# Own buffers for the second layer's sums and the last results, and the next pair's factors prepared later

## The chip, the core and the metric

The kernel runs on one core of a Trainium2 chip. The metric is the device time of one execution in microseconds (us). Five engines take part, each with its own queue of instructions that it works off in order: TensorE (PE, matrix products, with its weight loads shown as PEld), VectorE (DVE), ScalarE (ACT), GpSimd (POOL) and SyncE (SP), whose queue issues most of the transfers. They meet only at semaphores: an instruction that waits holds up everything behind it on its engine.

## What is computed

```python
def _attn_ref(q, k, v, omega):            # Performer attention, 4 batches, 8 heads, 576 x 64
    q_p, k_p = (phi(q * scale), phi(k * scale))      # random features, exp
    kv = np.einsum('bhsm,bhsd->bhmd', k_p, v)
    num = np.einsum('bhsm,bhmd->bhsd', q_p, kv)
    den = np.einsum('bhsm,bhm->bhs', q_p, np.sum(k_p, axis=2))[..., None] + 1e-06
    return num / den

def _moe_ref(x, w_in, w_out):             # layer one, 2304 tokens, 512 -> 2048 -> 512
    h = x @ w_in
    return (h * np.clip(h + 3.0, 0.0, 6.0) / 6.0) @ w_out

def _moe2_ref(x, w_in, w_out):            # layer two, same sizes
    h = x @ w_in
    return (h / (1.0 + np.exp(-1.702 * h))) @ w_out
```

The result is layer two of layer one of the attention's output.

## The kernel before

All products are in float32, each factor split into a high and a low part: a "split" is a cast on ACT (the high part) and a subtraction on DVE or POOL (the low part), and every product of two factors is then three matmuls. Attention of one batch runs beside layer one of the batch before it. Layer one writes its result to `xs` in DRAM; layer two reads it from there. The change lies in layer two and in the preparation of its input.

**Layer two, first half (`h_pair`).** The four batches are worked on in two pairs. For each pair, the product with the 2048 columns of `w_in` is made in eight steps (u = 0 to 7), each by Strassen's scheme: seven products instead of eight, `product(op, ...)` with op 1, 6, 2, 5, 7, 3, 4 in this order, of six matmuls each. Their left factors (sums and differences of weight blocks) come from DRAM through the six buffers `wss`; their right factors `xo` are sums and differences of blocks of the input, split. Four PSUM banks take a step's products: b1 (op 1, then op 2), b6 (op 6), b5 (op 5, then op 3), b7 (op 7, then op 4). Steps alternate between the two groups of four banks, `acc` and `psp`. DVE adds them up (L856): u2, t, and the sums c22, c12 and c21. `gated` (L863, L864) makes the activation of a block: a sigmoid on ACT, then a product on POOL for c22, c12 and c21, on DVE for b1. The results g stay in SBUF.

**Layer two, second half (`o_block`).** For each of the pair's two batches, 16 chunks of 128 rows of g are split (`halves`: L931 on ACT, L932 on DVE) into a buffer `gs`, and twelve matmuls for each chunk (L921) add to four banks (`o`); the first batch of a pair uses the banks `acc`, the second `psp`. At the end of a block `evict` brings the banks to SBUF and they are sent out. The last block of the program also does the rest, 64 rows of each batch that do not fill a tile: two banks more, which are evicted first, in halves of 128 KB.

**Buffers.** A pool's tag is a ring of buffers: a new tile of a tag waits until the readers of the tile that held its buffer are done. The tag `gs` of the pool `gp`, three buffers, holds the chunks' splits, and also c22, c12 and c21 of every step of `h_pair`. The pool `lp` has a tag `gs` too, three buffers, which only the rest's smaller splits use. `evict` takes its buffer from `ga` (three) and `ob` (two) in turn.

**The next pair's factors (`x_ops`).** While the first pair's `o_block`s run, 16 steps prepare the second pair's xo: for each of two halves q a load of two tiles `xr` from `xs` (a ring of two buffers, so the second load waits for the first half's last readers), and seven parts in the order op 1, 2, 3, 7, 6, 5, 4. A part of op 7, 6, 5 or 4 makes its sum in place on POOL (L615 to L621), and then splits it: L623 on ACT, L624 on DVE. `side` takes one step after each chunk.

**What sets the order.** The instructions are written in the order of the Python code, but a scheduler then places them, engine by engine, by its own estimate of when each can run: an instruction that is ready early moves ahead. So the place of a split or a matmul in its queue follows from when its buffer comes free. Transfers of weights for later items (`fetch_to`, L757 and L760) are issued from SP, up to five items ahead.

Of the kernel before, what the change touches and what calls it, by code (L numbers as in the profile page):

```python
# [22 lines left out]
def performer_moe_kernel(  # L23
# [23 lines left out]
    SM = R * P  # L47
# [513 lines left out]

    n_out = [0]

    def evict(ps, sc, wide):
        n_out[0] += 1
        k = n_out[0]
        tag, bufs = ("ga", 3) if wide and k % 2 else ("ob", 2)
        ob = gp.tile([P, SM], F32, tag=tag, bufs=bufs, name="ob")
        if k % 2:
            nc.vector.tensor_scalar(out=ob, in0=ps, scalar1=sc, scalar2=None, op0=ALU.mult)  # L570
        else:
            nc.scalar.activation(out=ob, in_=ps, func=AF.Copy, scale=sc)
        return ob
# [15 lines left out]
    def x_ops(p, pool, tag):  # L589

        raw = {}
        room = {}

        def place(k):
            if 4 <= k < 10:
                return lp.tile([P, 2, SM], F32R, tag=f"xo{k - 4}", name="xo")
            if k in (0, 10):
                room[k] = xp_.tile([P, 4, 2, SM], F32R, tag="x", bufs=2, name="xo")
            return room[0][:, k] if k < 4 else room[10][:, k - 10]

        def load(q):
            for e in range(2):
                t = raw[q, e] = pool.tile([P, 2, SM], F32, tag=tag, bufs=2, name="xr")
                nc.sync.dma_start(
                    out=t, in_=xs[2 * p + e].rearrange("(h q) p s -> q p h s", q=2)[q]
                )

        def part(q, k, op):
            (b11, b21), (b12, b22) = (
                (raw[q, e][:, 0], raw[q, e][:, 1]) for e in range(2)  # L610
            )
            add = nc.gpsimd.tensor_tensor
            src = {1: b11, 2: b21, 3: b22, 7: b12, 6: b11, 5: b12, 4: b21}[op]
            if op == 7:
                add(out=b12, in0=b22, in1=b12, op=ALU.subtract)  # L615
            elif op == 6:
                add(out=b11, in0=b12, in1=b11, op=ALU.add)
            elif op == 5:
                add(out=b12, in0=b22, in1=b11, op=ALU.subtract)
            elif op == 4:  # L620
                add(out=b21, in0=b21, in1=b11, op=ALU.subtract)  # L621
            s = xop[q, op] = place(k)
            nc.scalar.copy(s[:, 0], src)  # L623
            nc.vector.tensor_tensor(out=s[:, 1], in0=src, in1=s[:, 0].bitcast(F32), op=ALU.subtract)  # L624

        order = (1, 2, 3, 7, 6, 5, 4)
        steps = []
        for q in range(2):
            steps.append(lambda q=q: load(q))
            steps += [lambda q=q, k=k: part(q, 7 * q + k, order[k]) for k in range(7)]  # L630
        return steps

    omt = const.tile([P, M], F32, name="omt")
# [104 lines left out]
    def side():  # L738
        pace[1] += 1
        if pace[1] % 2:  # L740
            return
        while todo and (pace[0] - len(todo)) * 4 * NC < pace[0] * pace[1]:
            todo.pop()()
# [69 lines left out]
    def h_pair(p, u):  # L813
# [35 lines left out]
        def bank():  # L849
            return psum.tile([P, SM], F32, tag=tag, name="h")  # L850

        def temp(tag, bufs, name):
            return gp.tile([P, SM], F32, tag=tag, bufs=bufs, name=name)

        def add(out, a, b):
            nc.vector.tensor_tensor(out=out, in0=a, in1=b, op=ALU.add)  # L856
# [10 lines left out]
        w["a"] = next_item()  # L867
        b1, b6 = bank(), bank()
        product(1, "a", 0, b1, True)
        p1 = temp("ga", 3, "p1")  # L870
        nc.scalar.copy(p1, b1)
        w["d"] = next_item()
        product(6, "d", 0, b6, True)
        u2 = temp("ga", 3, "u2")
        add(u2, p1, b6)
        product(2, "a", 1, b1, False)
        gated(0, b1, nc.vector)
# [3 lines left out]
        w["c"] = next_item()  # L881
        b5, b7 = bank(), bank()
        product(5, "c", 1, b5, True)
        t = temp("ga", 3, "t")
        add(t, u2, b5)
        product(7, "c", 0, b7, True)
        c22 = temp("gs", 3, "c22")
        add(c22, t, b7)
        product(3, "d", 1, b5, False)
        c12 = temp("gs", 3, "c12")  # L890
        add(c12, u2, b5)
        w["b"] = next_item()
        gated(2, c12, nc.gpsimd)
        gated(3, c22, nc.gpsimd)
        product(4, "b", 1, b7, False)
        c21 = temp("gs", 3, "c21")
        add(c21, u2, b7)
        gated(1, c21, nc.gpsimd)
        if last:
# [11 lines left out]
    def o_block(p, e, side):  # L911
# [23 lines left out]
        for c in range(NC):  # L935
            w = next_item()
            if left:
                s = halves(lp, B * SL, gl[c // 4][:, c // 2 % 2, c % 2])
                for d in range(B * SL // P):
                    rows(s, w, pl[d], d, c)  # L940
                    if c == NC - 1:
                        ob = evict(pl[d], 1.0, True)
                        for k, eng in enumerate((nc.sync, nc.scalar)):
                            r0 = (2 * d + k) * S + SM
                            eng.dma_start(out=out[r0:r0 + SL, :], in_=ob[k * SL:(k + 1) * SL, :])
            s = halves(gp, SM, gt[c // 2, e][:, c % 2])
            for d in range(SM // P):
                rows(s, w, ps[d], d, c)
                if c == NC - 1:
                    ob = evict(ps[d], 1.0, True)  # L950
                    nc.sync.dma_start(out=out[i * S + d * P:i * S + (d + 1) * P, :], in_=ob)
            side()
# [8 lines left out]
    for p in range(B // 2):  # L961
# [4 lines left out]
        if p + 1 < B // 2:  # L966
            prep = x_ops(p + 1, l1, "xr") + [left_x]

        def side():
            if prep:  # L970
                prep.pop(0)()

        for e in range(2):
# [60 lines left out]
```

## Time and profile before

| | |
|---|---|
| median of 3 runs | 958.74 us (958.34 to 961.16) |
| the profiled execution, its own time | 957.59 us |
| its span, first to last instruction | 955.8 us |
| PE busy | 931.8 us, 97% of the span |
| DVE, ACT, POOL busy | 523.6, 441.8 and 261.9 us |
| mean granted TensorE clock | 0.995 of full speed |

The profiled execution takes 1.8 us more than its span, and 1.15 us less than the median. PE is busy nearly all the time, so time can only be lost where PE stands still, where its clock falls, or before its first and after its last matmul. Matmul durations overlap (one is shown with some 0.39 us, and starts follow each other at 0.23 us), so the pace is read from a stretch of many.

### The profile page before, as it was taken

What the parts mean: (1) busy time and instruction counts of PE and PEld (TensorE: products, weight loads), DVE (VectorE), ACT (ScalarE), POOL (GpSimd) and SP (SyncE); (2) the same over time, 40 slices, a digit from 0 to 9 for tenths busy, and PEclk for the clock granted to TensorE, in tenths of its full rate; (3) what the DMA queues carried; (4) which work ended last, traced back from release to release, by engine and by line L of the source; (5) the groups of instructions that cost most, each with busy time, mean ns of one, the idle gap of its engine ahead of it and who ended that gap; (6) DMA issues with size and microseconds to landing.
All of it is one profiled execution on the core that took longest, in us unless ns stands there. A gap on an engine that the chain in (4) does not pass through costs nothing.

```text
span 955.8 us, 14633 instructions
## 1 busy us (share of the span) xinstructions
PE 931.8 (97%) x5566; PEld 764.7 (80%) x5566; DVE 523.6 (55%) x879; ACT 441.8 (46%) x904; POOL 261.9 (27%) x223
## 2 busy tenths in 40 slices
PE   8899999999999999999999999998999999999997
PEld 7777777778887888878888888876888888878885
DVE  7888889587574766547554234448232433342221
ACT  5887676576553765636443233344222323232221
POOL 0112223055342454516441005346000233210000
PEclk9999999999999999999999999998999999999999
DMA  5668578688776786756553257674576555466531
GB/s 189 227 230 277 211 258 311 232 292 296 234 284 247 243 295 238 265 199 248 212 199 114 88 176 258 210 231 182 197 235 205 176 176 176 158 197 203 170 111 66
DMA packets 62101, 203.47 MB, mean 213 GB/s; under 512 B 6736, under 2 KB 8400, under 8 KB 62032
## 3 DMA queue, kind: packets, MB, share of 16 engines
q1 hardware_dynamic: 61872, 202.28, 62.0%
q8 instruction: 44, 0.72, 0.3%
q10 hardware_dynamic: 160, 0.26, 0.1%
q14 instruction: 25, 0.20, 0.1%
HBM read 155.85 MB, written 46.66 MB: 212 GB/s over the span
## 4 chain that ended last, share of the span: by engine, by line
PE 81%; DVE 9%; ACT 5%; DMA 2%; issue 1%; POOL 1%; SPq 0%; ACTq 0%; DVEq 0%; POOLq 0%
PE o L921 19%; PE ps L495 17%; PE o L545 17%; PE h L823 16%; PE ps L250 3%; DVE w L200 2%; PE hl L840 2%; PE ps L383 1%; PE ps L347 1%; POOL w L193 1%; ACT e L258 1%; ACT wtop L176 1%; DVE xo L624 1%; PE ps L369 1%; DVE mx L256 1%
## 5 line engine op out<-in xcount | busy, mean ns | idle before, releaser
L921 PE MATMUL o<-wss,gs 128*128 128x512 f32 x864 | 200.7, 394 | 5.8 <-ACT gs L931 4.7
L921 PEld LDWEIGHTS o<-wss,gs 128*128 128x128 f32 x864 | 163.5, 190 | 43.0 <-ACT gs L931 5.6
L823 PE MATMUL h<-xo,wss 128*128 128x512 f32 x672 | 159.0, 393 | 0.0
L545 PE MATMUL o<-gs,wss 128*128 128x512 f32 (+1 forms) x660 | 150.5, 375 | 1.5 <-ACT gs L511 1.5
L495 PE MATMUL ps<-x,wss 128*128 128x512 f32 x576 | 145.8, 398 | 2.2 <-DVE x L240 0.7
L823 PEld LDWEIGHTS h<-xo,wss 128*128 128x128 f32 x672 | 124.5, 188 | 26.9
L193 POOL TENSOR_TENSOR w<-w,wpow 128x512 f32<-128x512 f32 x64 | 76.0, 1208 | 234.9 <-DVE wpow L188 152.7
L545 PEld LDWEIGHTS o<-gs,wss 128*128 128x128 f32 x660 | 112.4, 188 | 22.7 <-ACT gs L511 2.9
L495 PEld LDWEIGHTS ps<-x,wss 128*128 128x128 f32 x576 | 104.2, 188 | 26.1 <-ACT wss L203 1.6
L864 POOL TENSOR_TENSOR g<-g,c 128x512 f32<-128x512 f32 x48 | 63.6, 1329 | 175.7 <-ACT g L863 175.2
L932 DVE TENSOR_TENSOR gs<-g,gs 128x512 fp32r<-128x512 f32 x64 | 48.6, 764 | 102.0 <-ACT gs L931 101.7
L507 DVE SCALAR_TENSOR_TENSOR ga<-ga,ps 128x512 f32<-128x512 f32 (+1 forms) x80 | 49.9, 628 | 86.4 <-ACT ga L506 86.2
L931 ACT CAST gs<-g 128x512 fp32r<-128x512 f32 x64 | 39.6, 621 | 108.0 <-PE o L921 104.8
L506 ACT ACTIVATE ga<-ps,three 128x512 f32<-128x512 f32 (+1 forms) x80 | 51.8, 651 | 74.4 <-PE ps L495 74.4
L200 DVE TENSOR_TENSOR w<-w,wtop 128x512 f32<-128x512 f32 x64 | 70.0, 1106 | 20.9 <-POOL w L193 20.5
L258 ACT ACTIVATE e<-ps,mx 128x128 f32<-128x128 f32 x220 | 62.9, 396 | 19.1 <-DVE mx L256 19.1
L545 PE MATMUL o<-gs,wsh 128*128 128x512 f32 (+1 forms) x300 | 68.8, 376 | 1.2 <-ACT gs L511 1.2
L512 DVE TENSOR_TENSOR gs<-ga,gs 128x512 fp32r<-128x512 f32 (+1 forms) x80 | 59.2, 754 | 19.5 <-ACT gs L511 18.3
L863 ACT ACTIVATE g<-c 128x512 f32<-128x512 f32 x48 | 30.3, 632 | 73.1 <-DVE c L856 73.1
L545 PEld LDWEIGHTS o<-gs,wsh 128*128 128x128 f32 x300 | 51.4, 188 | 11.2 <-ACT gs L511 1.4
L511 ACT CAST gs<-ga 128x512 fp32r<-128x512 f32 (+1 forms) x80 | 45.9, 582 | 16.1 <-DVE ga L507 15.9
L220 POOL TENSOR_TENSOR wsn<-w,wsn 128x512 fp32r<-128x512 f32 x32 | 42.7, 1334 | 31.4 <-ACT wsn L219 31.4
(152 smaller groups left out, 1204.1 us busy)
## 6 DMA issues: line engine op xcount, KB each, us to landing
wss<-ws1o SPq DMA_DIRECT2D x64, 512.0 KB, 3.3
wss<-ws0i SPq DMA_DIRECT2D x36, 512.0 KB, 4.9
wss<-ws0o SPq DMA_DIRECT2D x33, 512.0 KB, 4.8
wraw<-in_w_in_dram SPq DMA_DIRECT2D x32, 512.0 KB, 4.6
wraw<-in_w_out_dram SPq DMA_DIRECT2D x32, 512.0 KB, 5.7
ws1o<-wsn SPq DMA_DIRECT2D x16, 512.0 KB, 3.5
wss<-sumsa SPq DMA_DIRECT2D x16, 512.0 KB, 3.4
wss<-sumsd SPq DMA_DIRECT2D x16, 512.0 KB, 3.7
```

The costliest lines, as they stand in the source:

```text
L193: nc.gpsimd.tensor_tensor(out=w[:, cols], in0=w[:, cols], in1=q[:, cols], op=ALU.mult)
L200: nc.vector.tensor_tensor(out=wj, in0=wj, in1=a[:, j * DM:(j + 1) * DM], op=ALU.add)
L258: act = nc.scalar.activation(out=e[:, r, :], in_=ps[:, r, :], func=AF.Exp, bias=mx[:, r:r + 1])
L495: nc.tensor.matmul(out=ps, lhsT=w[:, wi, kk, :], rhs=x[:, xi, kk, :], start=(m == 0), stop=(m == 3 * NK - 1),)
L506: nc.scalar.activation(out=g, in_=ps, func=AF.Relu, bias=three)
L507: nc.vector.scalar_tensor_tensor(out=g, in0=g, scalar=6.0, in1=ps, op0=ALU.min, op1=ALU.mult)
L512: gate[1] = nc.vector.tensor_tensor(out=s[:, 1, :], in0=g, in1=s[:, 0, :].bitcast(F32), op=ALU.subtract)
L545: nc.tensor.matmul(out=ps[:, e, :], lhsT=w[:, wi, cols], rhs=s[:, gi, :], start=(c == 0 and m == 0 and per == 1), stop=(c == NC - 1 and m ...
L823: nc.tensor.matmul(out=ps, lhsT=s[:, wi, q, :], rhs=xop[q, op][:, xi], start=(first and m == 0), stop=(m == 5), skip_group_check=not first,)
L864: eng.tensor_tensor(out=g, in0=g, in1=src, op=ALU.mult)
L921: nc.tensor.matmul(out=ps, lhsT=s[:, gi, d * P:(d + 1) * P], rhs=w[:, wi, :], start=(c == 0 and m == 0), stop=(c == NC - 1 and m == 2),)
L932: nc.vector.tensor_tensor(out=s[:, 1], in0=g, in1=s[:, 0].bitcast(F32), op=ALU.subtract)
```

## The change

The three sums c22, c12 and c21 take their buffers from the tag `gs` of `lp` instead of that of `gp`. The rest's two results take theirs from `lp`'s tags `xo0` and `xo1` (factors that are no longer read then) instead of `ga` and `ob`. In `x_ops` a sum on POOL is written one step ahead of the split that uses it, and `side` lets two chunks pass before its first step.

```diff
-    def evict(ps, sc, wide):
+    def evict(ps, sc, wide, home=None):
         n_out[0] += 1
         k = n_out[0]
-        tag, bufs = ("ga", 3) if wide and k % 2 else ("ob", 2)
-        ob = gp.tile([P, SM], F32, tag=tag, bufs=bufs, name="ob")
+        if home is not None:
+            ob = lp.tile([P, SM], F32, tag=home, name="ob")
+        elif wide and k % 2:
+            ob = gp.tile([P, SM], F32, tag="ga", bufs=3, name="ob")
+        else:
+            ob = gp.tile([P, SM], F32, tag="ob", bufs=2, name="ob")
...
-        def part(q, k, op):
-            (b11, b21), (b12, b22) = (
-                (raw[q, e][:, 0], raw[q, e][:, 1]) for e in range(2)
-            )
+        def quarters(q):
+            return [raw[q, e][:, h] for h in range(2) for e in range(2)]
+
+        def total(q, op):
+            b11, b12, b21, b22 = quarters(q)
             add = nc.gpsimd.tensor_tensor
-            src = {1: b11, 2: b21, 3: b22, 7: b12, 6: b11, 5: b12, 4: b21}[op]
             if op == 7:
...
+        def part(q, k, op):
+            b11, b12, b21, b22 = quarters(q)
+            src = {1: b11, 2: b21, 3: b22, 7: b12, 6: b11, 5: b12, 4: b21}[op]
             s = xop[q, op] = place(k)
...
-            steps += [lambda q=q, k=k: part(q, 7 * q + k, order[k]) for k in range(7)]
+            for k in range(7):
+                def step(q=q, k=k):
+                    part(q, 7 * q + k, order[k])
+                    if 2 <= k < 6:
+                        total(q, order[k + 1])
+                steps.append(step)
...
-        c22 = temp("gs", 3, "c22")
+        c22 = temp(lp, "gs", "c22")
...
-                        ob = evict(pl[d], 1.0, True)
+                        ob = evict(pl[d], 1.0, True, f"xo{d}")
...
+        wait = [2]
+
         def side():
-            if prep:
+            wait[0] -= 1
+            if prep and wait[0] < 0:
                 prep.pop(0)()
```

c12 and c21 change as c22 does. The numbers of all instructions stay the same; their order changes on every engine around the ends of `h_pair`.

PE at the end of the first pair's `h_pair`, before (h_6895 is b5 of the last step, h_6896 its b7; o_6938 to o_6941 are the first block's four banks; gs_6944, gs_6965 its first chunks' splits):

```order
L823 MATMUL h_6896<-xo_6088,wss_6798 128x512 x3
L823 MATMUL h_6895<-xo_5792,wss_6786 128x512 x3
L823 MATMUL h_6895<-xo_6020,wss_6786 128x512 x3
L823 MATMUL h_6896<-xo_5941,wss_6817 128x512 x3
L823 MATMUL h_6896<-xo_6088,wss_6817 128x512 x3
L921 MATMUL o_6938<-wss_6845,gs_6944 128x512 x2
L921 MATMUL o_6939<-wss_6845,gs_6944 128x512 x2
L921 MATMUL o_6940<-wss_6845,gs_6944 128x512 x2
L921 MATMUL o_6941<-wss_6845,gs_6944 128x512 x2
```

And in the changed kernel (gs_6944, gs_6961 and gs_6978 are the first three chunks' splits, gs_6999 the fourth's):

```order
L836 MATMUL h_6896<-xo_6088,wss_6798 128x512 x3
L934 MATMUL o_6938<-wss_6845,gs_6944 128x512 x3
L934 MATMUL o_6938<-wss_6862,gs_6961 128x512 x3
L836 MATMUL h_6895<-xo_5792,wss_6786 128x512 x3
L836 MATMUL h_6895<-xo_6020,wss_6786 128x512 x3
L934 MATMUL o_6939<-wss_6845,gs_6944 128x512 x3
L934 MATMUL o_6939<-wss_6862,gs_6961 128x512 x3
L836 MATMUL h_6896<-xo_5941,wss_6817 128x512 x3
L836 MATMUL h_6896<-xo_6088,wss_6817 128x512 x3
L934 MATMUL o_6938<-wss_6874,gs_6978 128x512 x3
L934 MATMUL o_6939<-wss_6874,gs_6978 128x512 x3
L934 MATMUL o_6940<-wss_6845,gs_6944 128x512 x3
```

Matmuls of the block's first three chunks now stand between and behind the last two products of the step (op 3 and op 4), where before the block began only behind both; then follow 15 more of these chunks, and the fourth's.

ACT at the same place, before (c22_6911, c12_6919 and c21_6934 are the last step's sums; xr and xo the next pair's):

```order
L863 ACTIVATE g_6923<-c12_6919 128x512
L623 CAST xo_7059<-xr_6959 128x512
L863 ACTIVATE g_6890<-c21_6934 128x512
L931 CAST gs_6944<-g_6358 128x512
L931 CAST gs_6965<-g_6358 128x512
L623 CAST xo_7101<-xr_6959 128x512
L623 CAST xo_7080<-xr_6961 128x512
```

And in the changed kernel:

```order
L631 CAST xo_7014<-xr_6995 128x512 x2
L876 ACTIVATE g_6923<-c12_6919 128x512
L631 CAST xo_7093<-xr_6993 128x512
L876 ACTIVATE g_6890<-c21_6934 128x512
L631 CAST xo_7135<-xr_6993 128x512
L631 CAST xo_7114<-xr_6995 128x512
L944 CAST gs_6999<-g_6434 128x512
L944 CAST gs_7019<-g_6510 128x512
```

The casts of the first three chunks have gone from here to the second step of `h_pair`, some 60 us earlier; the first cast of the block at this place is the fourth chunk's, and it stands behind all seven of the first half's xo. DVE's splits stand in the same order as ACT's casts, with the four xo_7014 ahead of c21_6934 where three were before.

## Rows read from the trace of the kernel before

**Rows 1.** The page's line of busy times and shares.

```profile
PE 931.8 (97%) x5566; PEld 764.7 (80%) x5566; DVE 523.6 (55%) x879; ACT 441.8 (46%) x904; POOL 261.9 (27%) x223
```

**Rows 2.** Stretches: length, then busy time (instructions) per engine; granted clock, DMA share, GB/s.

```profile
565.50:643.18 77.68, 77.68 (x337) 62.75 (x335) 32.02 (x50) 27.73 (x47) 31.11 (x26) 1.00 0.73 233
643.18:647.30 4.12, 0.01 (x2) 0.01 (x1) 4.12 (x6) 2.95 (x6) 3.97 (x3) 0.79 0.84 312
648.00:650.00 2.00, 2.00 (x6) 1.56 (x5) 2.00 (x2) 0.64 (x2) 2.00 (x3) 0.50 0.00 0
647.30:661.45 14.15, 13.99 (x50) 11.04 (x51) 11.45 (x11) 5.76 (x11) 8.23 (x6) 0.82 0.43 163
661.45:665.45 4.00, 3.06 (x13) 2.18 (x13) 4.00 (x4) 2.33 (x5) 3.29 (x3) 1.00 0.68 232
668.24:738.90 70.66, 70.66 (x312) 58.40 (x312) 20.35 (x31) 16.45 (x27) 0.00 (x0) 1.00 0.63 208
```

**Rows 3.** PE in order of time: start, length, work, [idle before it, releaser].

```profile
636.80 6.38 PE L823 MATMUL h<-xo,wss 128*128 128x512 f32 x27
647.30 14.00 PE L921 MATMUL o<-wss,gs 128*128 128x512 f32 x50 [4.11 <-ACT gs L931]
661.45 3.06 PE L921 MATMUL o<-wss,gs 128*128 128x512 f32 x12 [0.16 <-DVE gs L932]
665.45 2.79 PE L921 MATMUL o<-wss,gs 128*128 128x512 f32 x11 [0.94 <-DVE gs L932]
```

**Rows 4.** ACT around the end of the first pair's `h_pair`, in order of time.

```profile
641.13 1.66 ACT L623 CAST xo<-xr 128x512 fp32r<-128x512 f32 x3 [1.91 <-PE h L823]
646.64 0.61 ACT L931 CAST gs<-g 128x512 fp32r<-128x512 f32 x1
648.30 0.62 ACT L931 CAST gs<-g 128x512 fp32r<-128x512 f32 x1 [1.06 <-POOL g L864]
```

**Rows 5.** DVE there, in order of time.

```profile
639.69 0.68 DVE L864 TENSOR_TENSOR g<-g,h 128x512 f32<-128x512 f32 x1
641.91 0.69 DVE L856 TENSOR_TENSOR c<-u,h 128x512 f32<-128x512 f32 x1 [0.71 <-PE h L823]
642.51 2.96 DVE L624 TENSOR_TENSOR xo<-xr,xo 128x512 fp32r<-128x512 f32 x3
645.39 0.67 DVE L856 TENSOR_TENSOR c<-u,h 128x512 f32<-128x512 f32 x1
648.75 3.44 DVE L932 TENSOR_TENSOR gs<-g,gs 128x512 fp32r<-128x512 f32 x2
...
667.61 0.68 DVE L932 TENSOR_TENSOR gs<-g,gs 128x512 fp32r<-128x512 f32 x1
```

**Rows 6.** POOL there, in order of time; then its product L864 from 565 to 640 us.

```profile
643.33 1.59 POOL L617 TENSOR_TENSOR xr<-xr 128x512 f32<-128x512 f32 x1 [4.24 <-issue]
644.88 3.39 POOL L864 TENSOR_TENSOR g<-g,c 128x512 f32<-128x512 f32 x2
...
L864 POOL TENSOR_TENSOR g<-g,c 128x512 f32<-128x512 f32 x21 | 27.0, 1294 | 31.5 <-ACT g L863 31.2
```

**Rows 7.** PE at the end of the second pair's `h_pair`.

```profile
836.10 2.94 PE L823 MATMUL h<-xo,wss 128*128 128x512 f32 x12
839.67 10.72 PE L921 MATMUL o<-wss,gs 128*128 128x512 f32 x46 [0.63 <-ACT gs L931]
```

**Rows 8.** The program's end: SP's issues of results, the last evictions on DVE and ACT.

```profile
948.50 4.22 SPq L951 DMA_DIRECT2D out_dram<-ob x4
949.16 0.69 DVE L570 TENSOR_SCALAR ob<-o 128x512 f32<-128x512 f32 x1 [0.68 <-PE o L921]
951.77 0.60 ACT L572 ACTIVATE ob<-o 128x512 f32<-128x512 f32 x1 [2.50 <-DMA out_dram<-ob]
```

**Rows 9.** POOL and ACT in the first pair's first steps.

```profile
580.54 5.06 POOL L864 TENSOR_TENSOR g<-g,c 128x512 f32<-128x512 f32 x4
583.61 0.59 ACT L871 COPY p<-h 128x512 f32<-128x512 f32 x1
```

More of the change, by code (lines that the diff above doesn't have):

```diff
@@ L850, in bank, with temp @@
             return psum.tile([P, SM], F32, tag=tag, name="h")
-        def temp(tag, bufs, name):
-            return gp.tile([P, SM], F32, tag=tag, bufs=bufs, name=name)
+        def temp(pool, tag, name):
+            return pool.tile([P, SM], F32, tag=tag, bufs=3, name=name)
         def add(out, a, b):
@@ L869, in h_pair @@
         product(1, "a", 0, b1, True)
-        p1 = temp("ga", 3, "p1")
+        p1 = temp(gp, "ga", "p1")
         nc.scalar.copy(p1, b1)
@@ L873, in h_pair @@
         product(6, "d", 0, b6, True)
-        u2 = temp("ga", 3, "u2")
+        u2 = temp(gp, "ga", "u2")
         add(u2, p1, b6)
@@ L883, in h_pair @@
         product(5, "c", 1, b5, True)
-        t = temp("ga", 3, "t")
+        t = temp(gp, "ga", "t")
         add(t, u2, b5)
         product(7, "c", 0, b7, True)
-        c22 = temp("gs", 3, "c22")
+        c22 = temp(lp, "gs", "c22")
         add(c22, t, b7)
         product(3, "d", 1, b5, False)
-        c12 = temp("gs", 3, "c12")
+        c12 = temp(lp, "gs", "c12")
         add(c12, u2, b5)
@@ L895, in h_pair @@
         product(4, "b", 1, b7, False)
-        c21 = temp("gs", 3, "c21")
+        c21 = temp(lp, "gs", "c21")
         add(c21, u2, b7)
```

## The prediction

> **What bounds the kernel now.** I read the page's shares first: PE is busy for 97% of the span, and DVE, ACT and POOL for 55% and less [rows 1]. So an engine beside PE matters only where PE waits for it. Cutting layer two into stretches shows where that is. From 565.50 to 643.18 us PE does the first pair's `h_pair` without a gap, 336 matmuls in 77.68 us, 0.2312 us each; from 668.24 to 738.90 it does 312 of the block that follows, 0.2265 us each, again without a gap [rows 2]. Between them lies the loss. PE in order of time names it [rows 3]: after the last matmul of `h_pair` (636.80 + 6.38 = 643.18) it stands for 4.11 us until a cast L931, later for 0.16 and 0.94 us until subtractions L932.
>
> Why the cast is late stands in ACT's and POOL's rows. The second chunk's cast waits 1.06 us for POOL's product L864 [rows 4], and the first one comes in the moment at which POOL's first product of 644.88 us is done (644.88 + 1.70 = 646.6) [rows 4, 6]. What they have from each other is the buffer: the split of a chunk needs one of the three `gs`, and c22, c12 and c21 of the last step hold all three until POOL has multiplied them. POOL is late in turn since it made a sum of the next pair first (643.33, 1.59 us), and c21 is late since DVE ran three splits of the next pair (2.96 us) ahead of it [rows 5, 6].
>
> The stop costs more than its length. Behind it the granted clock is at 0.50, the lower of its two levels (1.2 GHz): 6 matmuls in 2 us instead of nearly 9 [rows 2]. The 50 matmuls up to 661.45 take 14.15 us where the later pace gives 50 x 0.2265 = 11.33, so 2.82 us are lost there. The next 12 take 4.00 us instead of 2.72: 1.28. With the stop of 4.12 the loss is 8.22 us; in other words, matmul 63 of the block starts at 665.45 instead of 643.18 + 62 x 0.2265 = 657.22.
>
> **The change part by part.**
>
> *Sums in buffers of their own.* With `gp`'s three `gs` free since layer one, the first three chunks' splits move to the second step of `h_pair`, and PE can begin the block before its last two products. I replay the new order from the end of op 7, in the time of the old trace. Op 3 and op 4 are 12 matmuls, so op 7 ends at 643.18 - 12 x 0.2312 = 640.41. The first six block matmuls need b1's product on DVE, which was over at some 640.4: I allow 0.1. Then: six of the block to 641.9, op 3 to 643.3, six to 644.6, op 4 to 646.0, six to 647.4, nine into the third bank to 649.4, nine into the fourth. The third bank was b5 and needs c12 read: DVE can do that at 643.3 (0.69 us), in time. The fourth was b7 and needs c21.
>
> c21 stands behind four splits of the next pair. The ACT casts begin when op 3 is done with the old factor, half-way through, at 642.6; the first split follows c12 at 644.0 and takes 0.7. The other three run beside POOL. The last two of the three in the trace took (2.96 - 0.68) / 2 = 1.14 us each when POOL worked beside them for part of the time, and two subtractions 1.72 each when it did all the time; with POOL idle one takes 0.68 [rows 5, 6]. I take 1.4, so c21 starts at 648.9 and ends at 649.6, 0.2 us after PE wants the bank. The bounds: at 1.14 it is in time; at 1.72 PE stands 1.2 us.
>
> *The fourth chunk* is what is late next. Its buffer is free when the first chunk's last matmul is done (about 650.3), but ACT has the casts of op 6, 4 and 5 ahead of its cast, and the last of these waits for POOL's last sum. POOL's chain is: sum 6, which waits for the first split (644.7); the product for c12; sum 4; sum 5. Under contention POOL's steps took 1.59 to 1.70 us, alone 1.29 [rows 6]; four of 1.68 end at 651.5. Two casts of 0.62 follow, so the fourth chunk is split at 652.75. PE would want it at 647.4 + 18 x 0.2265 = 651.45: a wait of 1.3 us, which contains the 0.2 above. From below it is 0 (POOL at 1.3: 651.15), from above 2.4 (below, with the rivals). The later chunks are ready two chunks ahead, since a buffer comes free every 2.7 us and a split takes 1.3.
>
> *The clock.* PE's waits of 0.94 and 0.16 us left it at 1.00, the stop of 4.12 did not [rows 2, 3]. I take it that 1.3 us leave it at 1.00; if not, 2.8 us come back.
>
> So matmul 63 starts at 640.41 + 0.1 + 12 x 0.2312 + 62 x 0.2265 + 1.3 = 658.6. **Gain: 665.45 - 658.6 = 6.85 us.**
>
> *The second pair.* At 839.04 PE stands 0.63 us for a cast [rows 7]. No next pair is prepared there, so DVE and POOL are free: c21 after the last product has six us until its bank is wanted, and the fourth chunk's cast waits for one product of POOL (1.3) only. **Gain 0.6**; bounds 0.3, and 0.9 as the twelve matmuls before took 2.94 us instead of 2.77 [rows 7].
>
> *The rest's results.* The last eviction, on ACT, starts at 951.77 after 2.50 us of waiting for a transfer out of `ob` [rows 8]: the rest's second result had that buffer. With buffers of its own it starts as soon as the last matmul is done, three matmuls behind the third bank's end of some 949.1, at 949.8, so 1.95 us earlier. The last transfer then follows two others of 256 KB by some 0.4 us each, where it went alone before (SP's issues run until 948.50 + 4.22), and shares the engines with them; I take off 0.5. **Gain 1.4**, bounds 0.8 and 1.95.
>
> *Casts moved ahead.* In the second step ACT now casts the second and third chunk behind POOL's product for the first c21. That was the third of four in 5.06 us from 580.54, so done at 584.3 [rows 9]. ACT's copy of the next b1, at 583.61 before, moves to 586.1, behind two casts and a sigmoid of 0.6. PE wants it after op 1, 6, 3 and most of 5 and 4 of other banks, some 24 matmuls or 5.5 us after the copy's old start: 589.1. The copy ends at 586.7, so 2.4 us are left, and it costs nothing.
>
> *Sums a step ahead, two chunks later.* POOL's and SP's queues keep their contents. On SP the second half's two loads, one of which waits for the split of op 4 and the other for that of op 5, now have weights of chunks 6 to 8 between them. The splits end at some 651.5 and 653; chunk 7 is wanted after 660, so the cover is 7 us. Counted at nothing.
>
> **Sum:** 6.85 + 0.6 + 1.4 = 8.85 us off the profiled execution's own 957.59: 948.7. The runs' median is 1.15 us above that execution, so 949.8.
>
> **The rivals.**
>
> 1. *DVE and POOL take turns.* If a split waits for a whole step of POOL, three splits cost 3 x (0.68 + 1.29) = 5.9 us instead of 4.2. Then c21 ends at 651.3, PE stands 1.9 us at the fourth bank, and the sum for op 5, which overwrites what the fourth split reads, begins at 650.6. The fourth chunk comes at some 653.8: 2.4 us lost instead of 1.3, so 950.9; and if the clock falls behind it, another 2.8: 953.7. For it: the trace's 1.72 us for a subtraction of 0.68. Against it: a subtraction and a step of POOL took 1.72 together, less than 1.97. The Trainium skill, "SBUF — State Buffer", section "SBUF: two separate sides", says that VectorE with two SBUF inputs and GpSimd lock a port pair for a whole instruction, while the other is blocked. By that rule the time would be this rival's 950.9; the trace agrees in direction, but shows less than the full sum.
>
> 2. *The stop only moves.* The splits of the next pair are as many as before, and stand ahead of the fourth chunk's. If their chain takes until 657 instead of 652.75, PE stands 5 us there, the clock falls, and of the first gain nothing is left: 958.74 - 0.6 - 1.4 = 956.7. For it: one chain of ACT, DVE and POOL still feeds PE. Against it: 30 matmuls (6.8 us) now cover it.
>
> 3. *Slower.* The copy of b1 in the first pair waits behind casts that wait for POOL. It decides from 2.4 us more delay on POOL's first products; past that PE stops, and a stop of 4 us or more takes the clock down. To eat all gains and end above 961.6 it must stop 8.9 us (with 2.8 for the clock, 8.85 + 2.9 in all). That needs POOL 11 us late; its four products took 5.06 [rows 9].
>
> **How the numbers follow.** Forecast 949.8: 0.73. Rival 1, at 950.9 to 953.7: 0.14. Rival 2, at 956.7: 0.09. Rival 3: 0.04. About 0.3% (2.9 us) can be told from no change, so the first two count as faster (0.87), rival 2 as the same (0.09), rival 3 as slower (0.04). The range: without any wait at the fourth chunk and with the upper bounds of the other two gains it is 949.8 - 1.3 - 0.3 - 0.55 = 947.6, and half a us is left for the spread: 947.1. Above it takes in rival 1: 954.0.
>
> **What would show it.** After: PE without a stop at the end of `h_pair`, but one of some 1.3 us at the fourth chunk, released by L944 on ACT; granted clock 1.00 from 643 to 660; the second block's start without the 0.63; the last eviction within 0.1 us of PE's end. It is wrong if the clock shows 0.50 behind the fourth chunk, or if c21 holds PE for over a microsecond.

## The result, and the profile after

The changed kernel takes 949.90 us (median of 4 runs, 949.11 to 950.91), the kernel before 958.88 us in the same measurement (958.34 to 961.16). The recorded ratio is 0.9911, with a 95% interval of 0.9899 to 0.9923 (the two medians divide to 0.9906, inside it). The forecast was 949.8 us. The profiled execution of the changed kernel takes 949.11 us, its span is 947.3 us, and its mean granted clock 0.999 of full speed instead of 0.995.

The page's line of busy times says little, as [rows 1] did: every engine has as many instructions as before, and PE is busy for 928.5 us instead of 931.8, since fewer of its matmuls ran at the lower clock.

The view of waits, for PE in layer two alone (560 to 956 us), has one row left. Its columns are who waited, for whom, the sum in us, how often, and the longest.

```profile
PE o L934 <- ACT gs L944: 1.1, 1, 1.1
```

PE in order of time at the end of the first pair's `h_pair` (start, length, work, idle before it and releaser) shows the place of that wait, and answers to [rows 3]:

```profile
635.78 4.31 PE L836 MATMUL h<-xo,wss 128*128 128x512 f32 x18
639.93 1.75 PE L934 MATMUL o<-wss,gs 128*128 128x512 f32 x6
641.52 1.56 PE L836 MATMUL h<-xo,wss 128*128 128x512 f32 x6
642.92 1.55 PE L934 MATMUL o<-wss,gs 128*128 128x512 f32 x6
644.31 1.56 PE L836 MATMUL h<-xo,wss 128*128 128x512 f32 x6
645.70 5.77 PE L934 MATMUL o<-wss,gs 128*128 128x512 f32 x24
652.55 16.64 PE L934 MATMUL o<-wss,gs 128*128 128x512 f32 x72 [1.08 <-ACT gs L944]
```

The block's matmuls (L934) now begin before the last two products (L836), in groups of six as the order showed, and the stop of 4.11 us is gone. What is late is the fourth chunk, by 1.08 us. The clock stays up behind it. In the two stretches below (columns: length; PE, PEld, DVE, ACT and POOL busy with their instructions; granted clock; DMA share; GB/s) it is 1.00, where [rows 2] had 0.50 and 0.82:

```profile
643.00:655.00 12.00, 10.92 (x48) 8.42 (x47) 11.54 (x12) 6.12 (x12) 8.40 (x5) 1.00 0.60 186
652.55:668.28 15.73, 15.73 (x69) 13.03 (x70) 12.51 (x14) 7.46 (x13) 6.67 (x5) 1.00 0.80 285
```

Why the fourth chunk is late stands in the other engines' rows, in order of time. First ACT, then DVE, then POOL (answering to [rows 4 to 6]):

```profile
642.41 2.19 ACT L631 CAST xo<-xr 128x512 fp32r<-128x512 f32 x4 [0.87 <-PE h L836]
...
651.36 0.62 ACT L631 CAST xo<-xr 128x512 fp32r<-128x512 f32 x1 [1.07 <-POOL xr L623]
651.89 1.66 ACT L944 CAST gs<-g 128x512 fp32r<-128x512 f32 x3
```

```profile
643.19 0.69 DVE L869 TENSOR_TENSOR c<-u,h 128x512 f32<-128x512 f32 x1 [2.31 <-PE h L836]
643.79 4.68 DVE L632 TENSOR_TENSOR xo<-xr,xo 128x512 fp32r<-128x512 f32 x4
648.40 0.67 DVE L869 TENSOR_TENSOR c<-u,h 128x512 f32<-128x512 f32 x1
```

```profile
644.61 1.62 POOL L621 TENSOR_TENSOR xr<-xr 128x512 f32<-128x512 f32 x1 [1.71 <-issue]
646.19 1.74 POOL L877 TENSOR_TENSOR g<-g,c 128x512 f32<-128x512 f32 x1
647.89 1.75 POOL L625 TENSOR_TENSOR xr<-xr 128x512 f32<-128x512 f32 x1
649.60 1.73 POOL L623 TENSOR_TENSOR xr<-xr 128x512 f32<-128x512 f32 x1
```

POOL's four steps (a sum, the product for c12, two sums) follow each other without a gap from 644.61 to 651.33. ACT's last cast for the next pair (651.36) waits for the fourth of them, and the fourth chunk's cast comes right behind it: it starts at 651.89 and lets PE go at 652.55. c21, which the fourth bank needs, is ready on DVE at 649.07 and holds nobody up.

At the second pair's end of `h_pair`, PE's row of the block has no idle time ahead of it (in [rows 7] there were 0.63 us):

```profile
833.77 8.58 PE L934 MATMUL o<-wss,gs 128*128 128x512 f32 x37
```

At the program's end the last eviction, on ACT, no longer waits for a transfer, but for PE (compare [rows 8]); SP's four issues, the last of which sends what this eviction made, take 2.87 us instead of 4.22:

```profile
940.47 2.87 SPq L964 DMA_DIRECT2D out_dram<-ob  x4
941.80 0.60 ACT L576 ACTIVATE ob<-o 128x512 f32<-128x512 f32 x1 [0.57 <-PE o L934]
```

**Where the time went.** From one execution to the next, the start of `h_pair` moves by up to 2.7 us, sometimes by five (last section), for reasons ahead of this point. So traces are compared here in stretches that count from PE's first matmul of the first pair's `h_pair`: to the first matmul L840 or L853 (`hl`, the second pair's first product with the rest), from there to the end of the last matmul, and from there to the end of the span. Spans are printed in tenths, so a tail is good to some 0.05 us.

| kernel | `h_pair` starts | first pair | second pair | tail | span |
|---|---|---|---|---|---|
| before | 565.34 | 173.44 | 211.02 | 6.0 | 955.8 |
| after | 565.06 | 166.53 | 210.17 | 5.5 | 947.3 |
| difference | -0.28 | -6.91 | -0.85 | -0.46 | -8.5 |

The four differences add up to 8.50 us; the two profiled executions differ by 957.59 - 949.11 = 8.48 us.

### The profile page after: what moved, and what is told of

It is laid out like the page before. It is cut to its first block, busy times and chain, and to the rows that moved or that the text cites. A ratio compares the mean times of both kernels' runs of the same rounds, so it can differ in the third digit from the quotient of the medians.

```text
span 947.3 us, 14614 instructions
## 1 busy us (share of the span) xinstructions
PE 928.5 (98%) x5566; PEld 762.5 (80%) x5566; DVE 521.0 (55%) x879; ACT 441.9 (47%) x904; POOL 261.6 (28%) x223
## 4 chain that ended last, share of the span: by engine, by line
PE 78%; DVE 9%; ACT 6%; POOL 2%; DMA 2%; issue 2%; SPq 0%; POOLq 0%; ACTq 0%; DVEq 0%
PE o L934 20%; PE h L836 16%; PE o L545 16%; PE ps L495 15%; DVE w L200 3%; PE hl L853 2%; PE ps L250 2%; POOL w L193 2%; ACT e L258 2%; ACT wtop L176 1%; PE ps L383 1%; PE ps L347 1%; DVE mx L256 1%; DVE wtop L184 1%; DMA sumsa<-wsn 1%
## 5 line engine op out<-in xcount | busy, mean ns | idle before, releaser
L934 PE MATMUL o<-wss,gs 128*128 128x512 f32 x864 | 198.7, 391 | 1.1 <-ACT gs L944 1.1
L934 PEld LDWEIGHTS o<-wss,gs 128*128 128x128 f32 x864 | 161.9, 188 | 36.8 <-ACT gs L944 1.5
L836 PE MATMUL h<-xo,wss 128*128 128x512 f32 x672 | 159.5, 393 | 0.0
L836 PEld LDWEIGHTS h<-xo,wss 128*128 128x128 f32 x672 | 124.6, 188 | 27.0
L945 DVE TENSOR_TENSOR gs<-g,gs 128x512 fp32r<-128x512 f32 x64 | 46.6, 734 | 101.0 <-ACT gs L944 101.0
```

Of the source, the lines that this page charges most:

```text
L836: nc.tensor.matmul(out=ps, lhsT=s[:, wi, q, :], rhs=xop[q, op][:, xi], start=(first and m == 0), stop=(m == 5), skip_group_check=not first,)
L934: nc.tensor.matmul(out=ps, lhsT=s[:, gi, d * P:(d + 1) * P], rhs=w[:, wi, :], start=(c == 0 and m == 0), stop=(c == NC - 1 and m == 2),)
L945: nc.vector.tensor_tensor(out=s[:, 1], in0=g, in1=s[:, 0].bitcast(F32), op=ALU.subtract)
```

## The experiments

Three questions were open. Which of the edits brings the gain? Is the ring of buffers the cause, or the next pair's work that stands ahead of the chunks' splits in ACT's and DVE's queues? And what is the rest of 1.08 us, and the small gain at the end, made of? Each kernel was measured against the kernel before on the same chip; ratios are to it. The expectations go by 958.9 us for the kernel before; in these measurements it took 958.3 to 958.6.

### One edit alone

The sums in `lp`'s buffers and nothing else of the change (kernel before with this edit; the fourth argument, new here, names the pool):

```diff
-        c22 = temp("gs", 3, "c22")
+        c22 = temp("gs", 3, "c22", lp)
```

and c12 and c21 alike.

> The kernel before with one edit: c22, c12 and c21 in the buffers of lp. Theory A (the shared ring alone makes the stop): PE's two stops at the ends of h_pair go, the fourth chunk waits about 1.1 us as in the changed kernel, since the next pair's splits stand in the same places; 958.9 - 6.9 - 0.8 = 951.2 (950.4 to 952.0). Theory B (the later factors are needed as well): the splits of the next pair hold the block up for longer, with the clock at 0.50 again; 954 to 957.

Measured: 951.79 us (950.88 to 952.52), ratio 0.9931 (0.9917 to 0.9944). PE's waits in layer two are those of the changed kernel to the tenth:

```profile
PE o L921 <- ACT gs L931: 1.1, 1, 1.1
```

Its first pair takes 166.58 us and its second 210.17: both gains of the changed kernel, 6.9 and 0.85 us, come from this edit alone. What it lacks is the end: its tail is 6.05 us. That is 0.5 of the 1.9 us by which its median lies above the changed kernel's; in the trace the other difference is the start of `h_pair` (566.30 instead of 565.06), which the edit does not touch, and the intervals of the two ratios overlap.

The rest's results in buffers of their own, and nothing else (with the new argument of `evict` as in the change):

```diff
-                        ob = evict(pl[d], 1.0, True)
+                        ob = evict(pl[d], 1.0, True, f"xo{d}")
```

> The kernel before with one edit: the rest's two results in buffers of their own. Theory A (the transfers at the end are the bound; the changed kernel ended 0.46 us earlier behind its last matmul): 958.4 (958.0 to 958.8), the last eviction at once behind the last matmul, the last transfer landing 1.0 us later after its issue than before. Theory B (the prediction's term): 957.5.

Measured: 957.84 us (11 runs, 956.27 to 961.65), ratio 0.9999 (0.9989 to 1.0008). The trace has what the edit is to do, the last eviction at once behind PE:

```profile
949.18 0.60 ACT L575 ACTIVATE ob<-o 128x512 f32<-128x512 f32 x1 [0.57 <-PE o L924]
```

and the tail is 5.35 us instead of 6.0. But so little does not show in the time: the interval reaches from a gain of 1.1 us to a loss of 0.8. That the edit is worth half a microsecond rests on traces: the tail is 5.3 to 5.7 us in the five of this study that have it (this one, after, and three below, with a mean of 5.48) and 5.8 to 6.05 in the five that do not (mean 5.97).

The factors prepared two chunks later and each sum a step ahead, without the buffers (the changed kernel with c22, c12 and c21 back in `gp` and the rest's results back in `ga` and `ob`):

```diff
-        c22 = temp(lp, "gs", "c22")
+        c22 = temp(gp, "gs", "c22")
...
-                        ob = evict(pl[d], 1.0, True, f"xo{d}")
+                        ob = evict(pl[d], 1.0, True)
```

> The kernel before with one edit: sums a step ahead of their splits and the first step two chunks later. Theory A (the splits run as soon as their data and buffers allow, whatever the chunk after which they are written): 958.9 (958.2 to 959.6), the stop of 4.1 us, the clock of 0.50 and three splits ahead of c21 as before. Theory B (later factors free DVE and POOL): the stop is 1 to 3 us shorter, 954 to 957.

Measured: 957.86 us (10 runs), ratio 0.9991 (0.9980 to 1.0003), and PE's waits are those of before:

```profile
PE o L934 <- ACT gs L944: 4.8, 2, 4.1
PE o L934 <- DVE gs L945: 1.0, 1, 1.0
```

So this third of the change does nothing: the stop is still 4.1 us long. With the buffers it does nothing either, as the first pair takes 166.53 us with it (the changed kernel) and 166.58 without (the sums' buffers alone). `side` delays where the steps are written, but the splits of ops 1, 2 and 3 depend on nothing but loaded data and a free factor, and in the trace three of the next pair's splits (2.96 us) stand ahead of c21 again.

### The ring, or the queue?

If the cost is the next pair's splits in front, then the ring may stay as it was and the splits be tied behind the chunk's (the kernel before, with this edit; `behind` makes what is written in it stand after the given instruction on its engine):

```diff
-            nc.scalar.copy(s[:, 0], src)
-            nc.vector.tensor_tensor(out=s[:, 1], in0=src, in1=s[:, 0].bitcast(F32), op=ALU.subtract)
+            with behind(last_split[0]):
+                nc.scalar.copy(s[:, 0], src)
+            with behind(last_split[1]):
+                nc.vector.tensor_tensor(out=s[:, 1], in0=src, in1=s[:, 0].bitcast(F32), op=ALU.subtract)
```

where `halves` puts its cast and its subtraction into `last_split`.

> The kernel before, buffers shared as before, with one edit of another kind: every split of the next pair is queued behind the split of the chunk after which it is written. Theory A (the ring costs what it does because the next pair's splits and sums delay the products that free it): the first cast comes right behind c12's sigmoid, at some 643.3 instead of 646.6, PE stands 0.9 us instead of 4.1, the clock stays at 1.00: 958.9 - 7.2 = 951.7 (950.9 to 953). Theory C (sharing itself is the cost, so that without own buffers nothing is won): 957 to 959.

Measured: 950.30 us (950.01 to 950.77), ratio 0.9916 (0.9903 to 0.9930): as good as the change by the time, with the old buffers, and 1.4 us below what was expected. PE in order of time at the first and at the second pair's end of `h_pair`, then two of ACT's rows:

```profile
635.69 7.55 PE L826 MATMUL h<-xo,wss 128*128 128x512 f32 x32
643.99 56.28 PE L924 MATMUL o<-wss,gs 128*128 128x512 f32 x247 [0.75 <-ACT gs L934]
...
832.04 10.28 PE L924 MATMUL o<-wss,gs 128*128 128x512 f32 x44 [0.63 <-ACT gs L934]
```

```profile
642.68 0.63 ACT L866 ACTIVATE g<-c 128x512 f32<-128x512 f32 x1 [0.76 <-DVE c L859]
643.32 0.62 ACT L934 CAST gs<-g 128x512 fp32r<-128x512 f32 x1
```

The block still begins only behind the last product, as the ring forces, but the first chunk's cast runs at 643.32, right behind a sigmoid, where before it came at 646.64 [rows 4]. PE stands 0.75 us and from then on not at all until the second pair; the first pair takes 165.77 us, 0.76 less than in the changed kernel. So most of the 4.11 us needed the ring and the queue together. As the rows read, three things stood in a row: the buffers are held until POOL's product, POOL makes a sum of the next pair first, and DVE puts three splits ahead of c21. Either cut breaks the chain: freeing the buffers puts 30 matmuls in front of it, and the new order takes the next pair out of it. (POOL's sum and DVE's splits were not moved apart from each other.)

What the ring costs by itself is left in this run. It is the 0.75 us, and at the second pair, where no next pair is prepared and order edges have nothing to move, the whole wait of 0.63 us [rows 7]: the second pair takes 211.03 us, as before, and 210.17 with buffers of their own.

### How much of the loss was the clock's?

Fifteen matmuls with zeros behind the last product fill the stop, so that PE stays busy (the kernel before with this edit; it puts these matmuls into a bank that is free then, and nobody reads their result; `mm` is the last matmul of op 4):

```diff
+        if p == 0 and u == NC // 2 - 1:
+            z = oth.tile([P, SM], F32, tag=otag, name="z")
+            with behind(mm):
+                for _ in range(15):
+                    nc.tensor.matmul(
+                        out=z, lhsT=zero_r, rhs=zero_r[:, 0:1].to_broadcast([P, SM]), start=True, stop=True
+                    )
```

> The kernel before with 15 matmuls on zeros into a bank that is free then, behind the last matmul of the first pair's h_pair (15 x 0.2265 = 3.4 us inside the stop of 4.1). Theory A (2.8 us of the loss are the lower clock behind the stop): the clock stays at 1.00, the first real matmul comes at the same time as before, matmul 63 of the block 2.8 us earlier or as far as the splits let it: 956.1 (955.5 to 957.5). Theory B (behind the stop the splits pace PE, not its clock): 958.9.

Measured: 956.54 us (10 runs, 955.86 to 961.03), ratio 0.9983 (0.9970 to 0.9995). The first pair takes 171.66 us, 1.78 less than before. PE in order of time, then the stretch behind the zeros:

```profile
648.40 3.44 PE L901 MATMUL z<-zero_r 128*128 128x512 f32 x15
652.68 2.09 PE L929 MATMUL o<-wss,gs 128*128 128x512 f32 x8 [0.85 <-ACT gs L939]
655.96 15.25 PE L929 MATMUL o<-wss,gs 128*128 128x512 f32 x66 [1.19 <-DVE gs L940]
671.79 28.58 PE L929 MATMUL o<-wss,gs 128*128 128x512 f32 x124 [0.58 <-DVE gs L940]
```

```profile
651.84:672.00 20.16, 17.55 (x75) 13.95 (x76) 16.60 (x16) 9.24 (x17) 12.26 (x9) 1.00 0.59 199
```

The clock is at 1.00 throughout, with the block starting as late as ever. So it does fall because of the stop, as the prediction read [rows 2]. But only 1.8 of the 2.82 us come back. The 0.85 us is what the zeros left of the stop; behind it the faster PE runs into the splits and waits 1.19 and 0.58 us, where the slow one had waited 0.16 and 0.94 [rows 3]. That is 0.67 us more; the other 0.4 were not traced. What the clock costs and what the late splits cost overlap: taking the one away alone gives back less than its rows show.

### The last 1.08 us

The sums of the next pair on DVE instead of POOL (the changed kernel with this edit):

```diff
-            add = nc.gpsimd.tensor_tensor
+            add = nc.vector.tensor_tensor
```

> The changed kernel with the next pair's sums on DVE instead of POOL. Theory A (the fourth chunk waits for POOL's four steps of 1.7 us, stretched by DVE): DVE makes a sum in 0.7, the fourth chunk's cast comes before PE wants it and the stop of 1.08 us goes: 948.9 (948.3 to 949.6). Theory B (DVE is the one that is late, and more work on it makes c21 later): PE stops at the fourth bank instead, 950 to 952.

Measured: 948.21 us (947.58 to 949.33), ratio 0.9891 (0.9870 to 0.9913). PE's only wait in layer two, then DVE in order of time:

```profile
PE o L934 <- DVE gs L945: 0.2, 1, 0.2
```

```profile
643.94 1.89 DVE L632 TENSOR_TENSOR xo<-xr,xo 128x512 fp32r<-128x512 f32 x3
645.75 1.78 DVE L621 TENSOR_TENSOR xr<-xr 128x512 f32<-128x512 f32 x1
...
649.86 2.99 DVE L632 TENSOR_TENSOR xo<-xr,xo 128x512 fp32r<-128x512 f32 x3
```

Three splits take 1.89 us where POOL stands still until the third has begun, and 2.99 where it works beside the first; a sum takes 1.78 beside POOL, and 0.68 with POOL still (at 648.66). With POOL out of the chain, the wait is 0.18 us instead of 1.08, and the first pair takes 165.42 us, 1.1 less. So the fourth chunk did wait for POOL's four steps. By the times alone this could not be told, as the interval of the ratio overlaps with the changed kernel's.

The changed kernel with the splits tied behind the chunks' (the edit shown above for the kernel before):

> The changed kernel with every split of the next pair queued behind the split of the chunk after which it is written. Theory A: the fourth chunk's cast is the first behind c21's sigmoid, no stop of PE is left from h_pair to the end of the block: 949.9 - 1.1 = 948.8 (948.1 to 949.4). Theory B (the next pair's factors then come too late for the second h_pair, or the splits between the chunks slow them): 950 or more.

Measured: 949.81 us (949.63 to 952.78), ratio 0.9913 (0.9892 to 0.9933). In layer two PE does not wait once, and the first pair takes 165.11 us, 1.4 less than in the changed kernel: by the trace the edit does what was expected. The time does not show it; with 4 runs and an interval of 4 us, a gain of 1.1 to 1.4 us can neither be seen nor ruled out.

The changed kernel unedited, a second time, as the measure for these:

> The changed kernel itself once more, as the yardstick of the two kernels beside it: 949.9 (949.2 to 950.6). Its own trace again shows one wait of 1.1 us at the fourth chunk and an end of some 5.5 us behind the last matmul.

Measured: 950.44 us (6 runs, 949.72 to 955.04), ratio 0.9913 (0.9899 to 0.9927); the wait of 1.08 us stands at the same place. The two ratios differ by far less than their intervals are wide.

### The end

If the tail is bound by 256 KB results that are evicted shortly before PE's end, it helps to finish some banks earlier. Here the rest's last two chunks go ahead of the batch's last two, and these two are done bank by bank (the changed kernel with this edit):

```diff
+            if left and c == NC - 2:
+                early[c + 1] = next_item()
+            for c2 in () if not left or c == NC - 1 else (c, c + 1) if c == NC - 2 else (c,):
...
+            if left and c == NC - 2:
+                before_last = (s, w)
+                continue
             for d in range(SM // P):
+                if left and c == NC - 1:
+                    rows(before_last[0], before_last[1], ps[d], d, c - 1)
                 rows(s, w, ps[d], d, c)
```

> The changed kernel with another order at the end of the last block: the rest's last chunk before the last two chunks of the batch, and these two taken bank by bank, so that the results come out 1.36 us apart instead of 0.68. Theory A (the 1.57 MB of results that all come in the last 3 us of PE are the bound of the end): the last transfer runs nearly alone, the end comes 4 us after the last matmul instead of 5.5: 948.4 (947.8 to 949.2). Theory B (the last issue and its own landing are the bound): 949.9.

Measured: 950.10 us (6 runs, 948.58 to 953.70), ratio 0.9911 (0.9892 to 0.9930). The tail is 4.07 us instead of 5.54. The last rows of SP's queue and of ACT:

```profile
940.21 4.31 SPq L973 DMA_DIRECT2D out_dram<-ob  x4
943.56 0.60 ACT L576 ACTIVATE ob<-o 128x512 f32<-128x512 f32 x1 [2.12 <-DMA out_dram<-ob]
```

SP's four issues now spread over 4.31 us, while PE still works until 943.53, and the last eviction is again done right behind PE. The time is no better than the changed kernel's, though: in this profiled execution `h_pair` began 1.33 us later than in that of after, and PE waited 0.20 us for a transfer of weights, as it did for 0.16 us in the unedited repeat. Alone, the edit stays undecided.

Both edits together, the splits tied behind and the new end:

> The changed kernel with the next pair's splits queued behind the chunks' splits and with the results of the last block spread out. Theory A (both losses are real and add up: 1.4 us at the fourth chunk, 1.5 at the end, as the traces of e7 and e8 show from the start of h_pair on, while their times were blurred by layer one): 947.0 (946.2 to 948.0), no wait of PE in layer two, 4.1 us from the last matmul to the end. Theory B (the times of e7 and e8 tell that neither brings anything): 949.9.

Measured: **947.24 us** (946.30 to 948.08), ratio 0.9882 (0.9867 to 0.9898), on the same chip as the repeated changed kernel: its slowest run is 1.6 us below the fastest of that one. PE from the start of the block:

```profile
645.97 84.51 PE L937 MATMUL o<-wss,gs 128*128 128x512 f32 x372
```

PE goes through layer two without a wait (first pair 165.13 us), and the tail is 4.03 us. This version beats both kernels, by 11.3 us and by 3.2. What neither edit showed alone shows in both: 1.4 and 1.5 us by the traces, 3.2 by the medians.

The sums on DVE and the new end:

> The changed kernel with the next pair's sums on DVE instead of POOL, and with the results of the last block spread out. Theory A: 949.9 - 1.1 - 1.5 = 947.3 (946.5 to 948.3). Theory B (the end of the program is bound by something that the spread doesn't touch): 948.2, as with the sums on DVE alone.

Measured: 947.87 us (946.40 to 948.62), ratio 0.9884 (0.9870 to 0.9899): not to be told from the one above. The first pair takes 165.28 us, with a wait of 0.2, and the tail is 3.65.

## Why the prediction was right, step by step

**What bounds the kernel.** The stop at the end of `h_pair`, the clock behind it and the late splits were read as 8.22 us of loss, with the buffers as the reason. Sums in `lp` alone end the stop (951.79), zeros in it end the fall of the clock (956.54). Only "what they have from each other is the buffer" was too narrow: in the first pair the chain could be cut at the queue just as well (950.30).

**First pair, 6.85 us: measured 6.91.** The parts hold too. The block begins between the products, in the predicted groups of six. c21 was to be late by 0.2 us with 1.4 us for each of the three splits behind the first; they took 4.01 us from the second one's start to c21's (644.39 to 648.40), 1.34 each, and c21 was ready 0.1 us before the 15th of the last 24 matmuls ended (645.70 + 15 x 0.2312 = 649.17). The fourth chunk was to cost 1.3 us and costs 1.08 of idle time. POOL's four steps were to take 1.68 us each, and took 6.72 together. The clock stayed at 1.00 behind a wait of that length.

That 1.4 us fits a split is partly luck, since none of the three took that long. One by one, on DVE:

```profile
644.39 0.69 DVE L632 TENSOR_TENSOR xo<-xr,xo 128x512 fp32r<-128x512 f32 x1
645.00 1.78 DVE L632 TENSOR_TENSOR xo<-xr,xo 128x512 fp32r<-128x512 f32 x1
646.70 1.77 DVE L632 TENSOR_TENSOR xo<-xr,xo 128x512 fp32r<-128x512 f32 x1
```

The first of these began before POOL's sum (644.61) and cost nothing extra; the other two each ended 0.55 us behind a step of POOL, and began 1.70 us apart, as POOL's steps did (646.19, 647.89, 649.60). The prediction's 1.14 from [rows 5] was such a mean too: the two splits took 0.69 and 1.75 us. Had all three run beside POOL at 1.70, c21 would have come some 1.0 us late by an estimate from these rows, near the prediction's bound of 1.2.

**Second pair, 0.6 us: measured 0.85,** just below the upper bound of 0.9, which counted besides the wait of 0.63 the slow twelve matmuls ahead of it [rows 7].

**Casts moved ahead, nothing: right.** ACT in the first pair's first steps:

```profile
584.53 1.14 ACT L944 CAST gs<-g 128x512 fp32r<-128x512 f32 x2 [2.08 <-POOL g L877]
586.11 0.57 ACT L884 COPY p<-h 128x512 f32<-128x512 f32 x1
```

The copy of b1, at 583.61 before [rows 9], comes at 586.11, behind the two casts and a sigmoid, to the tenth where the prediction had put it, and PE does not wait for it.

**Sums a step ahead, two chunks later, nothing: right,** and shown apart, with a ratio of 0.9991 and an unchanged stop.

**The rest's results, 1.4 us: measured 0.46, under the lower bound of 0.8. This is the step that failed,** by its size. "I take off 0.5" for the transfers that share the engines was too little. The last eviction does come earlier by what was said: 0.04 us behind the last matmul (941.76 to 941.80) instead of 1.97 (949.80 to 951.77), 1.93 against 1.95. From that 1.47 is lost again. About 0.52 goes in SP's queue: the four issues begin at 940.47, 941.84, 942.28 and 942.94, so the last one stands behind the third and begins 1.18 us behind PE's end where it was 2.59 (952.39), which is a gain of 1.41 and not of 1.93. The other 0.95 goes in the last transfer, which lands 3.0 us behind its issue where it took 2.0; from that landing to the end of the span it is 1.4 us in both. The stretches of 1 us behind PE's end (columns as above; DMA share and GB/s last) of after, and then of before:

```profile
941.80:942.80 1.00, 0.00 (x0) 0.00 (x0) 0.01 (x1) 0.60 (x1) 0.00 (x0) 1.00 0.96 293
942.80:943.80 1.00, 0.00 (x0) 0.00 (x0) 0.00 (x0) 0.00 (x0) 0.00 (x0) 1.00 0.99 369
943.80:944.80 1.00, 0.00 (x0) 0.00 (x0) 0.00 (x0) 0.00 (x0) 0.00 (x0) 1.00 1.01 387
```

```profile
951.80:952.80 1.00, 0.00 (x0) 0.00 (x0) 0.00 (x0) 0.56 (x1) 0.00 (x0) 0.97 0.61 234
952.80:953.80 1.00, 0.00 (x0) 0.00 (x0) 0.00 (x0) 0.00 (x0) 0.00 (x0) 0.50 0.60 225
```

Before, the last transfer had the engines to itself, at 60% of their time, and waited for no other. In the changed kernel it falls into a stretch in which the DMA engines are busy for 96 to 101% of their time, up to 944.80. So the end is no longer bound by an eviction but by SP's queue and by the bytes that are to go out behind PE's end, and that can't be seen from the wait that goes. The row that could have told it is the share of the DMA engines behind PE's end. Where results go out earlier (the new end above), 0.52 MB are moved behind PE's end instead of 1.15, and the tail is shorter by 1.5 us with the same eviction behind PE (4.07 against 5.54).

**The sum.** 6.91 + 0.85 + 0.46 = 8.22 us, against 8.85 forecast. That the median came within 0.1 us of the forecast is chance: the missing 0.63 us are made up by `h_pair`, which began 0.28 us earlier than in the profiled execution of before, and by the median, which lies 0.79 us above the profiled execution instead of 1.15. (The prediction's terms unrounded give 957.59 - 8.85 + 1.15 = 949.89.)

**The rivals.** The first, by which DVE and POOL take turns, has c21 at the end of 0.68 + 5.9 us of splits, 1.9 us too late for PE; it was in time. Its mechanism holds in part all the same: while both worked without a gap, one split went with each step of POOL. But such a pair took 1.70 us and not 0.68 + 1.29 = 1.97, and one of the three splits came before it. The Trainium skill, "SBUF — State Buffer", section "SBUF: two separate sides", has such a full lock; the trace shows the turns, at 0.27 us less for a pair than the sum of both steps. The second, that the stop only moves, is out: the chain ended at 652.5 and not at 657. The third, a slower kernel by b1's late copy, is out as well.

## What to carry to other kernels

When an engine waits for a buffer, follow who holds the buffer and what stands ahead of that holder in its queue: there may be two cuts. Here order edges alone did as much for the first pair as buffers of their own (165.77 against 166.58 us), but not for the second, where nothing stood ahead of the holder (211.03 against 210.17). A delay in program order does nothing where a scheduler may move independent work ahead of it. And before counting the full length of a wait that is removed at a program's end, look at whether the queue that issues the transfer and the DMA engines have room there for it when it comes earlier. And a mean over a few instructions can hide two kinds of them: look at each one before it becomes a price.

## What the runs showed of the hardware that was not expected

- In these traces DVE and POOL slow each other only in DVE's instructions with two inputs from SBUF. A DVE sum that reads one of its inputs from PSUM takes 0.67 us beside POOL (c21 at 648.40, while POOL works from 647.89 to 649.64), as it does alone. A split or a sum with two SBUF inputs takes 0.68 alone and up to 1.79 beside POOL, and POOL's step 1.29 alone and up to 1.76 beside such a step of DVE.
- In three of the thirteen profiled executions (the one with the zeros, the changed kernel with its splits tied behind, and its repeat) the granted clock falls in the first batch's attention, long before the place of the change. From 50 to 60 us it is 0.62 in the one with the zeros (first row) and 1.00 in after (second row). PE does 54 matmuls instead of 65, and `h_pair` starts at 570.72 instead of 565.06. The clock falls between 46 and 48 us, behind a wait of PE of 1.02 us for ACT that after has at the same place and with the same length. What decides it was not tried.

```profile
50.00:60.00 10.00, 10.00 (x54) 7.64 (x54) 5.28 (x14) 4.58 (x11) 2.27 (x2) 0.62 0.80 276
```

```profile
50.00:60.00 10.00, 9.08 (x65) 6.74 (x66) 9.26 (x19) 8.43 (x21) 2.27 (x2) 1.00 0.89 304
```

- Two losses behind one stop, the clock and the late splits, overlap: filling the stop gave back 1.8 us where the rows had shown 2.82 for the clock.
